# A planned order of 892 stages on one core: the old state added on VectorE, a square halved on GpSimd, and the last output row split

## The chip, the cores and the metric

The kernel runs on one core of one Trainium2 chip. The time is the device time of an execution in microseconds, and the figure that counts is the median of several executions. Five engines work beside each other and are bound to each other only by semaphores: PE (TensorE, matrix products), DVE (VectorE), ACT (ScalarE), POOL (GpSimd) and SP (SyncE, which here only issues transfers). Each runs its own instructions strictly in the order in which they were written.

## What is computed

Two layers follow each other. The first is a linear attention with a decaying state, for 4 batches, 8 heads, 768 time steps and a head size of 48. The second is a feed-forward layer from 384 to 1024 and back to 384, whose activation is h times softmax(h), followed by a layer norm.

```
state = 0
for t in range(S):
    cur = u * k[t] (outer) v[t]
    y[t] = r[t] @ (state + cur)
    state = w[t] * state + k[t] (outer) v[t]

h = y @ w_in                       # 3072 x 1024
solu = h * softmax(h)
ln = (solu - mean(solu)) / sqrt(var(solu) + 1e-6) * g_ln
out = ln @ w_out                   # 3072 x 384
```

## The kernel before, in words

The work is cut into 24 units: unit i is chunk c = i // 4 (128 time steps) of batch b = i % 4, with all 8 heads. A unit passes through about 35 small stages, and every stage is a Python function of a few instructions. What sets the order of everything is the string ORDER at the top of the file: 887 words, each a stage's short name, the unit's number and after a dot a choice. `Y13.i4`, for example, is the stage `attend` (Y) of unit 13, in form i, with PSUM bank 4; `kr2.d` is `transposed_copy` of unit 2 on DVE. The last lines of the kernel function walk through the words and call the stages. Each call goes through a small class (`InOrder`, its line 86 is what the profile gives for nearly every instruction), which ties each instruction to the one before it on the same engine, so that ORDER's order is the order on the engine; transfers issued by ACT and SP are kept in the words' order among each other too.

The stages that matter here, in the order in which one unit passes through them:

- LW, LK, LR, LV load w, k, r, v (192 KB each); the letter says whether SP (none), ACT (a) or POOL (g) issues the transfer.
- lw (ACT) takes the logarithm of w, cum (PE) sums it along time by two triangular products, ex (ACT) takes the exponential, kp (DVE) multiplies k and r with it. krk and krr (PE) transpose the results into PSUM, kr copies them to SBUF, on ACT or DVE. From unit 12 on, most units do this by a transposing transfer instead (kt, SP).
- p, q, dv (POOL) and dg (DVE) make the bonus term with u; vb casts v to bf16, on ACT or POOL.
- M (PE) makes the scores, m (mostly DVE) masks them into SBUF.
- Y (PE) makes y: old state times r, scores times v. In form i PE also adds the bonus term dv, by a product with the identity, and y is then copied by ACT; in form n it does not, and y is copied by DVE, which adds dv on the way.
- S (PE) adds the new part of the state in PSUM: a few tiny products for the decay, one product of the identity with the old state (384 columns, from chunk 1 on), and four products kp times v. et (ACT) takes the exponential of the decay, st (DVE) multiplies the sum with it and writes the new state in bf16, one of two buffers a batch.
- X (PE) transposes y and xT copies it to SBUF (ACT or DVE); some late units do this by a transposing transfer (xt, SP).
- H (PE) makes h, 24 products into two banks; e (ACT) is exp(h), he (DVE) is h times e, hq (ACT) is the square of he. In some late units ea (POOL) adds the two halves of e.
- Oa and Ob (PE) make the output for the first and the second four of the eight 128-row blocks of the hidden dimension: for each block one product of he with the weights (386 columns), one of e with a constant column (2 columns), and one of hq with a column of ones (1 column). In the units that have an ea, the e-products are only needed for every other block.
- qm (DVE), lv and rs (ACT) make the layer norm's factor, o (ACT or DVE) scales the row, out (SP) stores it. Units 17 to 20 use another form (ht), which does not matter here. Unit 23 makes its hidden part in two halves (HA to QB).

PSUM has eight banks, and the digit in a word says which one a stage takes; a stage that takes a bank waits until its last reader is done.

Of the kernel before, what the change touches and what calls it, by code (L numbers as in the profile page):

```python
# [21 lines left out]
LU0 LR3.g LW3.a LW1.a LW2.g lw3 LR0.a cum3.0 LG0 ih0 ex3 LW0 gs0.7 LK3 LR2.g hot1.2 LV0.g ik0 LK0 lw1 lw0 LV3.g
gc0 cum0.4 LK2.a us0.6 p0 lw2 LW5.g ex0 kp3 LR1 kp0 cum1.0 cum2.2 krk3.7 krr3 uc0 ex2 q0 ex1 kp2 LK1 LR6.g kp1
krk0.6 LW4 krr0 krk2.5 krr2 kr0.a lw4 LR4.g vb0.a kr2.d vb3.a p1 M0.3 p3 LO0 LW6 dg0 M2.5 kr3.a LK4 m0.d lw5
hot10.1 LV1 LR5 LK6.a dv0 LK5.g m2.d LV2.a LO1 M3.0 S0.7 q3 gw2.a gw3.a hot1.4 LI1 q1 lw6 krk1.6 cum4.2 et0 LV4
m3.d p2 st0 cum6.0 dg3 gw0.a cum5.4 ex4 S3.7 gw1.a p4 kp4 q2 dv3 krr1 ex6 dg1 LV5.g krk4.3 krr4 ex5 vb1.a Y0.i2
kp6 kr4.d y0.a LI2 et3 X0.2 krk6.3 st3 p6 kr1.a vb2.a LW8 xT0.a kp5 krr6 LI0.a dg2 M1.0 krk5.7 krr5 kr6.a m1.d
S1.2 dv1 M4.4 dv2 Y3.i3 S2.6 gw4.a LK7 gw7.a et2 kr5.d LW7.g et1 m4.d hot1.7 y3.a q4 gw6.a Y1.i3 M6.0 gw5.a st2
Y2.i5 y1.a y2.a vb5.a mn0.4 X2.7 wi0.a vb4.a st1 m6.d wi1.p LR7.g M5.2 X1.0 S5.1 xT2.a S4.6 et5 p5 lw7 LR8.g dg4
ce4.d LK8 LV7 et4 ce2.d wi2.a xT1.d st5 LW10.a st4 X3.5 m5.d LR10.a cum7.0 mc0 ex7 xT3.a ce1.d H0.6 dv4 H1.2 kp7  # L30
LK9.g H3.0 e0 lw8 e1 ce0.d LK10.a he0 he1 lw10 H2.6 ce7.d hq0.a ce3.p krk7.5 ce5.p e3 LV9 e2 LK11 hq1.a ce6.d
Oa0.3 q6 he3 vb7.a krr7 Ob0 LW9.g LV6.g Y4.i4 q5 LV8.g LR9.a he2 dg5 LW11 cum10.1 cum8.6 y4.a Oa1.0 qm0 ex10 lv0
rs0 kr7.d ex8 kp10 LW13.g Ob1 krk10.4 o0.a hq3.a p8 kp8 p7 dv5 Y5.n5 qm1 LR11.g y5.d lv1 M7.2 X4.6 LW15.a m7.d
q7 krr10 LW17 dg7 kr10.d xT4.a q8 dg6 rs1 lw11 p10 Oa3.5 o1.a cum11.6 dg8 hq2.a H4.2 LW12 LR12.a ex11 lw9 kp11
out0 S7.0 et7 Ob3 dv7 Y7.n1 vb6.a out1 cum9.6 LR17 LK15.g Oa2.4 qm3 st7 vb8.p e4 Ob2 he4 lv3 dv6 LK14.g krk8.0
S6.2 X5.3 LK12.a LV10 krr8 LV12.g ex9 lw13 y7.d rs3 o3.a hq4.a kp9 lw12 qm2 Y6.i5 lv2 xT5.d X7.7 krk11.6 LV11
vb9.p out3 kr8.d krr11 LR13.g LW14.a cum12.0 et6 xT7.a y6.a rs2 LR14.g st6 M8.2 krk9.5 krr9 kr11.d ex12 m8.a
H5.6 o2.d out2 q10 M11.3 LK13 lw17 kp12 dv8 LR15 S8.0 kr9.d LV15.g M9.1 e5 m11.d Oa4.5 LW18 Ob4 m9.a sel8 he5
LV14 et8 X6.6 vb11.a M10.3 st8 xT6.d p9 lw14 cum14.1 LK17.g hq5.a ex14 qm4 lv4 m10.d cum13.6 ex13 hot2.0 q9 rs4
kp14 kp13 dg9 Y8.i0 o4.a LW21.g dg10 sel9 Oa5.4 cum17.1 S9.3 LR16 lw15 p11 ex17 S11.5 cum15.6 Ob5 kp17 y8.a p12  # L40
et9 qm5 ex15 lv5 kp15 st9 dv9 Y9.n0 q11 q12 y9.d et11 rs5 H6.1 X8.6 o5.a p13 vb12.a p14 st11 dg11 kt12 e6 out4
dv11 LK21.g H7.3 X9.5 xT8.a he6 e7 LR19.g hq6.a vb10.a H8.6 lw18 krk14.0 LV16 dg12 krr14 dv10 kt15 xT9.d out5
he7 M12.1 Oa6.5 LV13.g Y11.n4 m12.d kr14.a e8 Ob6 M15.0 y11.d qm6 LR18 hq7.a lv6 he8 rs6 m15.d H9.3 dv12 o6.a
Y10.n2 y10.d e9 Oa7.7 he9 Ob7 LK19.g Y12.n0 S10.6 M14.2 LW16 X10.4 hq8.a LW22 y12.d qm7 xT10.d X12.5 Oa8.0 LV17
vb16.a out6 lw16 lv7 X11.1 LK16 hq9.a Ob8 xT12.a et10 p15 LR21 LK20.g LK18 cum16.4 m14.d q14 xT11.d cum18.2
vb14.a LR20.g dg14 rs7 st10 o7.a q15 qm8 S12.1 ex16 LW19.g LV18 LK22 H11.6 dg15 kp16 H12.4 vb15.p kt13 et12 ex18
lv8 vb13.p q13 e11 kp18 dv14 rs8 S15.2 o8.a S13.3 st12 e12 Oa9.0 dv15 he11 et15 lw21 LW20 Y15.n6 hq11.a et13
dg13 LV21 he12 Ob9 LV23.g LV19.g p18 st15 M13.4 LW23 y15.d qm9 dv13 kt16 cum21.1 hq12.a ex21 H10.6 lv9 p16 m13.d
st13 lw19 kp21 Y13.i4 Oa11.3 e10 rs9 o9.a out7 he10 q18 cum19.1 Ob11 dg18 qm11 lw20 Oa12.7 Ob12 ex19 LR22 q16
y13.a kp19 hq10.a M16.1 dg16 S14.5 lv11 Y14.n6 rs11 LV20.g X13.4 LV22.g out8 qm12 lv12 p17 m16.d xT13.d y14.d  # L50
o11.a lw22 S16.0 vb17.p et14 q17 dg17 rs12 st14 o12.a LR23 vb18.a cum20.1 p19 et16 ex20 ea10.p H13.3 q19 e13
xt15 dv17 lw23 kt17 dv16 H15.6 st16 kp20 he13 Oa10.5 xt14 M17.0 kt18 dg19 dv18 e15 cum22.2 Ob10 out9 ex22 vb22.p
Y16.i4 ea13.p he15 kp22 y16.a hq13.a p22 qm10 H14.6 vb20.p M18.3 m17.d p20 S18.2 q20 lv10 m18.d ea15.p e14 kt19
et18 rs10 Y17.n1 o10.a Oa13.0 y17.d kt20 p21 X16.4 Ob13 xT16.a st18 out11 q22 M19.3 xt17 he14 H16.1 hq15.a
Y18.n5 vb23.a e16 m19.d hq14.a Oa15.7 vb19.a dg20 kt21 y18.d qm13 out12 Ob15 ea14.p dv19 M20.4 q21 S17.3 lv13
he16 m20.d qm15 dv20 et17 hq16.a lv15 H17.1 rs13 out10 e17 M21.5 st17 xt18 rs15 ea16.p Oa14.4 m21.d Ob14 he17
o15.a o13.a cum23.5 qm14 LK23 Y20.n3 ex23 Y19.n7 lv14 y20.d y19.d H18.0 rs14 o14.a kp23 kt22 M22.3 e18 dg22
X20.2 vb21.p S19.7 m22.d xT20.a Oa16.6 Y21.n5 ht17 et19 p23 sv17 he18 xt19 hq17.a dv22 H20.2 e20 dg21 Ob16 st19
dv21 y21.d he20 hq18.a H19.0 qm16 e19 sv18 Y22.n4 Oa17.7 y22.d he19 kt23 Ob17 X22.5 sq17 M23.3 xT22.d qm17 m23.d
ht18 xt21 ht20 hq19.a lv16 Oa18.2 lv17 rs16 Ob18 ht19 q23 dg23 H21.0 o16.d sv19 Y23.n3 dv23 out15 hq20.a e21  # L60
y23.d H22.4 Oa20.6 out13 e22 Ob20 sq18 ea21.p Oa19.3 Ob19 he21 rs17 he22 hq21.a sq20 Oa21.1 o17.d sv20 out16
# [39 lines left out]
def kernel(  # L101
# [516 lines left out]
    def scaled_out(i, x):  # L618
        o_ps, rs, o = live[i]["o_ps"], rs_t[i % NWK], o_t[i % NWK]
        if x == "d":  # L620
            dve.tensor_scalar(out=o, in0=o_ps[:, :DM], scalar1=rs, scalar2=None, op0=MULT)
# [54 lines left out]
```

## Time and profile before

| what | value |
|---|---|
| median of 3 executions | 146.56 us (144.69, 146.56, 146.91) |
| the profiled execution, its own time | 145.05 us |
| its span from first to last instruction | 143.2 us |
| granted TensorE clock, mean | 0.995 |
| busy: PE / DVE / ACT / POOL | 127.6 / 124.0 / 122.2 / 117.2 us |
| bytes moved, mean rate | 31.67 MB, 221 GB/s |

The profile is of one execution. "Busy" is the time in which at least one record of an engine is open. Records of one engine overlap: the next instruction starts before the record of the one before it has ended, so the step from one start to the next is the better measure of what one more instruction costs. Matmuls are pipelined much more deeply than the rest, and there the difference is large. The view of stages gives, for each stretch of time, the busy time of each engine; the groups give mean durations; the timeline gives single instructions with the idle time before them and what ended it; the chain is followed back from the last instruction to what released each step.

### The profile page before, as it was taken

The numbers are of one execution on the slowest core, as the hardware profiler recorded it, in microseconds if no ns is written. First come the engines' busy times: TensorE is split into PE (matmuls) and PEld (weight loads), VectorE is DVE, ScalarE is ACT, GpSimd is POOL, SyncE is SP. The second block draws the span as 40 slices with busy tenths as digits, with TensorE's granted clock in tenths as the row PEclk, the third lists the DMA queues.
The fourth block names the chain that finished last, engine by engine and source line by source line (L and its number), as shares of the span: only waits on it lengthen the run. The fifth ranks groups of instructions, "written<-read, shape, count | busy, mean of one in ns | idle before, by whom it ended". The sixth has DMA issues, their size and how long they took to land.

```text
span 143.2 us, 4784 instructions
## 1 busy us (share of the span) xinstructions
PE 127.6 (89%) x1886; PEld 94.5 (66%) x1886; DVE 124.0 (87%) x206; ACT 122.2 (85%) x254; POOL 117.2 (82%) x150
## 2 busy tenths in 40 slices
PE   0597956988999999999999999996999999999980
PEld 0145445556967878678987797786778566687750
DVE  6048879979999999999999999999699999888480
ACT  3658799979999999999999989995787887887962
POOL 7999999999999999999999999999994753326000
PEclk9999999999999999999999999999999999999998
DMA  4999999999995999999998999996977863985325
GB/s 93 277 297 347 313 287 381 384 267 240 287 299 118 250 273 314 255 263 163 211 268 215 271 201 252 195 256 99 169 165 80 223 128 79 142 213 180 115 80 197
DMA packets 86488, 31.67 MB, mean 221 GB/s; under 512 B 80153, under 2 KB 84258, under 8 KB 86466
## 3 DMA queue, kind: packets, MB, share of 16 engines
q1 hardware_dynamic: 69330, 20.62, 66.6%
q0 software_dynamic: 2432, 7.47, 16.4%
q10 hardware_dynamic: 14704, 3.28, 10.5%
q8 instruction: 14, 0.23, 0.7%
q14 instruction: 8, 0.07, 0.1%
HBM read 22.03 MB, written 4.72 MB: 187 GB/s over the span
## 4 chain that ended last, share of the span: by engine, by line
PE 51%; POOL 21%; ACT 8%; issue 7%; DVE 5%; DMA 4%; ACTq 0%; POOLq 0%; DVEq 0%
PE ps L86 51%; DMA xT<-y 4%; POOL kr_in L86 4%; POOL p L86 4%; POOL q L86 3%; POOL dv L86 2%; POOL v_in L86 2%; ACT hq L86 2%; POOL w_in L86 2%; ACT e L86 2%; DVE he L86 1%; DVE o L86 1%; ACT o L86 1%; ACT ps L86 1%; DVE m L86 1%
## 5 line engine op out<-in xcount | busy, mean ns | idle before, releaser
L86 PE MATMUL ps<-w,he 128*128 128x386 bf16 (+1 forms) x192 | 42.5, 324 | 0.0
L86 PE MATMUL ps<-xT,win_sb 128*128 128x128 bf16 x480 | 29.6, 219 | 1.4 <-DMA xT<-y 1.2
L86 PEld LDWEIGHTS <-win_sb 128*128 128x128 bf16 x480 | 27.4, 98 | 3.0 <-DMA xT<-y 1.3
L86 POOL TENSOR_TENSOR dv<-vb,dg 128x384 bf16<-128x384 bf16 x24 | 19.8, 829 | 11.8 <-DVE dg L86 8.6
L86 DVE TENSOR_TENSOR kp<-ps,kr_in 128x768 bf16<-128x768 f32 x24 | 22.7, 953 | 6.9 <-DMA kr_in<-in_r_dram 3.8
L86 ACT ACTIVATE e<-ps 128x1024 bf16<-128x1024 f32 (+1 forms) x25 | 24.6, 987 | 4.8 <-PE ps L86 3.8
L86 DVE TENSOR_TENSOR m<-ps,keep 128x1024 bf16<-128x1024 f32 x22 | 26.7, 1218 | 0.9 <-PE ps L86 0.9
L86 DVE TENSOR_TENSOR he<-ps,e 128x1024 bf16<-128x1024 f32 (+1 forms) x21 | 24.5, 1170 | 3.0 <-ACT e L86 2.8
L86 PE MATMUL ps<-one_col,hq 128*128 128x1 bf16 x160 | 26.1, 163 | 0.0
L86 POOL TENSOR_TENSOR p<-kr_in 128x384 bf16<-128x384 f32 x24 | 23.9, 1005 | 0.1
L86 POOL TENSOR_TENSOR q<-p,u_bc 128x384 bf16<-128x384 bf16 x24 | 21.8, 916 | 0.3
L86 PEld LDWEIGHTS <-he 128*128 128x128 bf16 x192 | 18.3, 96 | 4.0
L86 ACT ACTIVATE hq<-he 128x1024 bf16<-128x1024 bf16 (+1 forms) x20 | 20.7, 1033 | 0.0
L86 ACT ACTIVATE ps<-ps 128x768 f32<-128x768 f32 x24 | 19.0, 800 | 1.5 <-PE ps L86 1.4
L86 PEld LDWEIGHTS <-hq 128*128 128x128 bf16 x160 | 14.1, 96 | 8.8
L86 PE MATMUL ps<-inv_col,e 128*128 128x2 bf16 x104 | 17.1, 164 | 0.0
L86 ACT ACTIVATE lw<-w_in 128x384 bf16<-128x384 f32 x24 | 12.3, 519 | 4.2 <-DMA w_in<-in_w_dram 4.2
L86 PEld LDWEIGHTS <-kp 128*128 128x128 bf16 x184 | 12.3, 101 | 4.2 <-DVE kp L86 1.9
L86 PEld LDWEIGHTS <-kr 64*128 64x128 bf16 (+1 forms) x272 | 10.2, 95 | 5.3 <-issue 2.1
L86 DVE TENSOR_REDUCE dg<-q 128x8 f32<-128x384 bf16 x24 | 12.9, 543 | 0.0
L86 DVE TENSOR_TENSOR st<-ps,et 128x384 bf16<-128x384 f32 x20 | 10.8, 551 | 1.4 <-ACT et L86 1.4
L86 POOL DMA_DIRECT2D v_in<-in_v_dram x12 | 10.9, 905 | 0.0
(97 smaller groups left out, 284.9 us busy)
## 6 DMA issues: line engine op xcount, KB each, us to landing
out_dram<-o SPq DMA_DIRECT2D x24, 192.0 KB, 2.7
w_in<-in_w_dram SPq DMA_DIRECT2D x12, 192.0 KB, 5.6
kr_in<-in_k_dram SPq DMA_DIRECT2D x12, 192.0 KB, 5.9
v_in<-in_v_dram POOLq DMA_DIRECT2D x12, 192.0 KB, 4.9
kr_in<-in_r_dram POOLq DMA_DIRECT2D x11, 192.0 KB, 4.5
v_in<-in_v_dram SPq DMA_DIRECT2D x11, 192.0 KB, 4.3
kr_in<-in_r_dram SPq DMA_DIRECT2D x9, 192.0 KB, 4.0
wout_f<-in_moe_w_out_dram SPq DMA_DIRECT2D x2, 768.0 KB, 7.1
```

What stands on the lines that cost most here:

```text
L86: made = make(*args, **kwargs)
```

## The change

ORDER is replaced by another one of 892 words. The same stages are called but for these:

- `S9.n3` and the like: in the units 9, 10, 13, 14, 18 and 19 the state's sum is made without the identity product of the old state. DVE adds the old state instead: it adds PSUM and the old state (bf16) into a new f32 buffer `sn` in SBUF, and then multiplies that buffer with the decay.
- `qa13.p` and the like: in the units 13, 14, 15, 16, 21 and 22 POOL adds the second half of hq to the first half (128x512), and Oa and Ob then need the one-column product for every other block only.
- `ea10.p` is gone: unit 10 makes all eight e-products again.
- `out23.h`: in the last unit ACT scales the left half of the row and DVE the right half, ACT and SP each store one half, and Ob23 runs all its he-products first, then those of e, then those of hq.
- Stages that change their engine: kr0, kr1, kr3, kr6 from ACT to DVE and kr2 from DVE to ACT; xT3, xT4, xT8 from ACT to DVE and xT1, xT11, xT13, xT22 from DVE to ACT; y6, y13 to DVE (form n), and y7, y14, y15, y17, y18 to ACT (form i, so with the identity product of dv); vb6, vb12, vb18, vb19 from ACT to POOL and vb17, vb21 from POOL to ACT; o2, o19, o20 from DVE to ACT and o18 from ACT to DVE.
- Many banks change, and nearly every compute stage stands at another place among its neighbours. In the word order the transfers of each issuing engine (SP 96, POOL 38, ACT 15) stand in the same order as before, apart from the split last store.

```diff
+    sn_t = ring("sn", 2, [C, H, D], F32)
...
-        s_ps = L["s_ps"] = bank([C, DM + H], F32, x, "s_ps")
+        s_ps = L["s_ps"] = bank([C, DM + H], F32, x[-1], "s_ps")
...
-        if c > 0:
+        L["apart"] = x[0] == "n"
+        if c > 0 and not L["apart"]:
             st = st_t[b][(c - 1) % 2]
             pe.matmul(s_ps[:, :DM], lhsT=ident, rhs=st.rearrange("p h e -> p (h e)"), start=False, stop=False,
                       skip_group_check=True)
...
-        dve.tensor_mul(out=st_t[b][c % 2], in0=live[i]["s_ps"][:, :DM].rearrange("p (h e) -> p h e", h=H), in1=et)
+        total = live[i]["s_ps"][:, :DM].rearrange("p (h e) -> p h e", h=H)
+        if live[i]["apart"]:
+            dve.tensor_add(out=sn_t[i % 2], in0=total, in1=st_t[b][(c - 1) % 2])
+            total = sn_t[i % 2]
+        dve.tensor_mul(out=st_t[b][c % 2], in0=total, in1=et)
...
+    def square_add(i, x):
+        hq = hq_t[i % NWK]
+        pool.tensor_add(out=hq[:, :KF // 2, :], in0=hq[:, :KF // 2, :], in1=hq[:, KF // 2:, :])
...
-            pe.matmul(o_ps[:, DM + 2:], lhsT=hq[:, f, :], rhs=one_col[:, :1], start=False, stop=(f == KF - 1),
-                      skip_group_check=True)
+            if i not in paired:
+                pe.matmul(o_ps[:, DM + 2:], lhsT=hq[:, f, :], rhs=one_col[:, :1], start=False, stop=(f == KF - 1),
+                          skip_group_check=True)
+            elif f % 2 == 0:
+                pe.matmul(o_ps[:, DM + 2:], lhsT=hq[:, f // 2, :], rhs=one_col[:, :1], start=False,
+                          stop=(f == KF - 2), skip_group_check=True)
...
+        if i == NU - 1 and split:
+            act.activation(out=o[:, :DM // 2], in_=o_ps[:, :DM // 2], func=COPY, scale=rs)
+            dve.tensor_scalar(out=o[:, DM // 2:], in0=o_ps[:, DM // 2:DM], scalar1=rs, scalar2=None, op0=MULT)
+            return
...
+        if x == "h":
+            act.dma_start(out=rows[:, :DM // 2], in_=o_t[i % NWK][:, :DM // 2])
+            sp.dma_start(out=rows[:, DM // 2:], in_=o_t[i % NWK][:, DM // 2:])
+            return
```

More of the change, by code (lines that the diff above doesn't have):

```diff
@@ L21 @@
 ORDER = """
[L22 to L61, printed above, removed]
@@ L62 @@
-hq22.a sq19 xt23 ea22.p out14 out17 qm18 qm20 qm19 lv18 HA23.5 rs18 o18.a EA23 DA23 lv19 HB23.7 rs19 out18 Ob21
-EB23 o19.d QA23.a qm21 DB23 lv20 QB23.d lv21 rs21 Oa22.4 Ob22 qm22 rs20 out19 Oa23.5 lv22 o21.d out21 rs22 o20.d
-Ob23 o22.a qm23 lv23 out22 rs23 out20 o23.a out23
+LU0 LW3.a LW1.a lw3 LR0.a LG0 LW0 lw0 LR3.g us0.0 LK3 gs0.5 cum3.2 gc0 uc0 LW2.g ih0 cum0.4 ex3 kp3 hot1.3 LR2.g
+LK0 LK2.a krk3.6 ex0 LV0.g ik0 lw2 cum2.2 kp0 LR1 LK1 ex2 LV3.g krk0.0 LW4 krr0 krr3 LO0 p0 LW6 kr3.d lw1 cum1.5
@@ new lines @@
+kp2 krk2.3 ex1 kr0.d LW5.g LK4 kp1 lw4 krr2 p2 LR6.g kr2.a vb0.a LV1 LR4.g M0.0 q0 hot1.4 M3.5 m0.d p3 krk1.4
+m3.d LR5 p1 lw5 LK5.g S0.0 q1 LK6.a krr1 LV2.a M2.6 dg0 gw3.a et0 q3 hot2.1 LO1 lw6 LI1 LV4 vb3.a kr1.d m2.d
+cum4.3 gw2.a cum5.6 ex4 cum6.1 q2 gw0.a LI2 dg3 LW8 dg2 kp4 hot10.5 ex6 dv0 st0 ex5 S3.0 kp6 et3 vb2.a dv3
+krk6.3 gw1.a LI0.a Y3.i1 p4 Y0.i5 LV5.g dg1 krr6 krk4.4 krr4 y3.a kp5 y0.a st3 kr6.d vb1.a gw4.a M1.1 q4 hot1.5
+dv2 dv1 Y2.i0 y2.a S2.7 LW7.g gw5.a m1.d M6.5 p6 wi1.p LR7.g p5 Y1.i0 m6.d gw6.a LR8.g S1.1 et2 LK7 dg4 LK8 LV7
@@ new lines @@
+kr4.d krk5.3 X2.2 st2 q6 krr5 gw7.a X3.5 y1.a vb4.a xT2.a LK9.g et1 kr5.d X1.4 xT1.a S4.0 M4.2 xT3.d X0.6 mn0.4
+st1 m4.d vb5.a wi0.a et4 M5.2 st4 ce2.d xT0.a lw7 wi2.a ce6.d LW10.a cum7.0 m5.d ce1.d LR10.a ce7.d dv4 mc0 S5.5
+lw8 ex7 H0.6 H1.2 kp7 e0 he0 ce4.d et5 H3.0 ce3.p e1 H2.6 LK10.a LV9 ce0.d krk7.4 st5 lw10 krr7 q5 he1 hq0.a
+LW9.g e3 e2 LV6.g ce5.p he3 Y4.i5 dg5 Oa0.3 hq1.a LK11 hq3.a he2 LV8.g LR9.a Ob0 qm0 cum10.1 ex10 Oa1.0 vb7.a
+cum8.6 LW13.g Ob1 p8 lv0 LW11 p7 y4.a rs0 o0.a kr7.d kp10 qm1 lv1 Oa3.5 ex8 q7 LW15.a LR11.g LW17 X4.4 M7.2 q8
@@ new lines @@
+LW12 Ob3 dg6 dg7 xT4.d vb9.p p10 vb6.p rs1 krk10.4 dv5 vb8.p lw11 kp8 krr10 LK15.g o1.a qm3 cum11.6 Y5.n1 hq2.a
+LR12.a ex11 lw9 LK14.g m7.d S7.0 lv3 lw17 dv7 H4.2 kr10.d lw12 y5.d kp11 et7 dg8 out0 st7 rs3 dv6 Oa2.4 e4 out1
+LV12.g cum9.6 LR17 LK12.a LV10 LR13.g he4 p11 krk8.1 LR14.g o3.a ex9 kp9 S6.0 krr8 et6 Ob2 LV11 Y7.i5 out3 q11
+krk9.2 lw13 lw15 kr8.d hq4.a X5.7 Y6.n3 LW14.a krk11.6 st6 LV15.g qm2 p9 dv8 krr11 y7.a lv2 rs2 o2.a cum12.0
+xT5.d y6.d out2 krr9 LK13 kr11.d ex12 X7.5 M8.3 kr9.d H5.6 kp12 m8.a LR15 LK17.g M11.3 xT7.a dg11 sel8 S8.0 M9.1
@@ new lines @@
+m11.d LW18 e5 Oa4.5 lw14 LW21.g he5 vb11.a et8 m9.a Ob4 X6.7 LV14 hq5.a st8 LR16 M10.3 xT6.d q9 dv11 m10.d
+cum14.1 cum13.6 q10 ex14 ex13 qm4 Y8.i0 kp14 kt12 Oa5.4 sel9 lv4 kp13 dg9 dg10 S9.n3 rs4 o4.a cum17.1 dv9 ex17
+S11.5 cum15.6 out4 kp17 y8.a Ob5 Y9.n0 LV16 ex15 qm5 vb10.a H6.1 lv5 et9 kp15 rs5 et11 p13 krk14.6 o5.a X8.7
+dv10 krr14 st9 p12 H7.3 e6 y9.d p14 kr14.a st11 X9.0 LK21.g LR19.g q12 xT8.d he6 H8.6 LV13.g e7 xT9.d hq6.a
+Y11.n2 M12.0 Oa6.5 he7 hq7.a e8 y11.d kt15 m12.d lw18 Ob6 dg12 out5 qm6 LR18 he8 vb12.p LW16 lv6 H9.2 rs6 LW22
@@ new lines @@
+vb14.a M15.0 Y10.n4 o6.a LV17 vb15.p m15.d S10.n7 out6 e9 Oa7.6 vb16.a he9 LK19.g Ob7 hq8.a Y12.n5 LK16 M14.1
+LR21 lw16 LK18 p15 LK20.g y10.d qm7 dv12 y12.d hq9.a lv7 rs7 LR20.g q15 LW19.g m14.d X10.4 Oa8.0 xT10.d et10
+dg15 vb13.p X11.5 Ob8 q13 LV18 st10 LK22 qm8 o7.a kt13 xT11.a lw21 X12.6 xT12.a cum16.4 p16 cum18.2 LW20 ex16
+lv8 dv15 LV23.g kp16 S12.1 LV19.g ex18 LV21 et12 H11.6 LW23 e11 kt16 out7 rs8 dg13 st12 H12.4 kp18 o8.a q14 e12
+q16 S13.n1 he11 cum21.2 Oa9.0 he12 Y15.i7 p18 hq11.a LR22 p19 out8 y15.a et13 st13 lw19 Ob9 qm9 M13.4 dv13 lv9
@@ new lines @@
+LV20.g H10.6 m13.d LR23 S15.1 ex21 xt15 e10 kt17 dg16 Oa11.5 vb17.a hq12.a Y13.n4 kp21 rs9 lw20 cum19.2 he10
+Ob11 y13.d ex19 qm11 Oa12.6 X13.4 o9.a Ob12 lv11 LV22.g p17 et15 dg14 xT13.a kp19 M16.2 st15 dv14 hq10.a q19
+rs11 S14.n7 cum20.0 o11.a Y14.i4 et14 y14.a qm12 vb20.p S16.5 dv16 lv12 et16 m16.d ex20 q18 H13.2 rs12 o12.a
+st14 dg19 Y16.i4 kp20 H15.6 e13 y16.a xt14 q17 lw22 st16 e15 kt18 p20 Oa10.5 dg17 he13 cum22.3 ex22 Ob10 hq13.a
+vb18.p M17.0 dg18 dv17 p21 he15 qm10 lv10 kp22 vb22.p dv18 out9 S18.n2 rs10 H14.6 ea13.p qa13.p et18 o10.a
@@ new lines @@
+hq15.a q21 M18.3 m17.d m18.d kt19 dg21 Y17.i5 kt20 X16.1 Oa13.0 y17.a xT16.a M19.4 st18 Ob13 out11 e14 H16.1
+lw23 Y18.i3 he14 xt17 e16 qm13 ea15.p m19.d qa15.p kt21 Oa15.7 vb19.p vb23.a he16 Ob15 dv19 ea14.p qm15 M20.5
+y18.a S17.4 lv13 m20.d hq14.a H17.1 et17 q20 M21.5 dg20 st17 Y19.n3 qa14.p hq16.a m21.d lv15 Oa14.4 rs13 e17
+out12 Ob14 dv20 rs15 out10 cum23.5 xt18 o13.a qa16.p he17 o15.a qm14 Y20.n7 p22 LK23 ea16.p ex23 kt22 p23 y19.d
+ht17 y20.d H18.0 lv14 e18 q22 vb21.a M22.2 kp23 X20.7 Oa16.6 rs14 xT20.a S19.n5 m22.d Ob16 sv18 dv21 H20.2 et19
@@ new lines @@
+he18 hq17.a q23 st19 dg22 xt19 dv22 kt23 e20 Y21.n7 o14.a y21.d dg23 qm16 H19.0 Y22.n5 ht18 Oa17.7 e19 he20
+y22.d Ob17 M23.4 xt21 ht20 X22.3 lv16 Oa18.2 he19 ht19 rs16 dv23 sq17 H21.0 m23.d hq20.a hq19.a xT22.a Y23.n4
+o16.d Ob18 H22.5 e21 sv17 hq18.a y23.d Oa20.4 Ob20 qm17 sq18 he21 qm18 e22 Oa19.3 ea21.p lv17 he22 sv19 lv18
+hq21.a rs17 out15 Ob19 sq20 out13 hq22.a o17.d out16 rs18 xt23 ea22.p sv20 sq19 HB23.1 HA23.6 qm20 qa21.p lv20
+out14 Oa21.0 qm19 EA23 qa22.p lv19 o18.d Ob21 DA23 rs20 rs19 o19.a out17 EB23 qm21 lv21 DB23 rs21 QA23.a Oa22.5
@@ L65 @@
+out18 Ob22 qm22 lv22 rs22 o21.d QB23.d o20.a o22.a Oa23.1 out19 out21 Ob23 qm23 out22 lv23 rs23 o23.d out20
+out23.h
 """
@@ L540, in hidden_square @@
             dve.scalar_tensor_tensor(out=hq, in0=he, scalar=EPS * EPS, in1=he, op0=MULT, op1=MULT)
+    paired = {int(word[2:].split(".")[0]) for word in ORDER.split() if word.startswith("qa")}
+    def square_add(i, x):
+        hq = hq_t[i % NWK]
+        pool.tensor_add(out=hq[:, :KF // 2, :], in0=hq[:, :KF // 2, :], in1=hq[:, KF // 2:, :])
     def hidden_half(part):
@@ L568 @@
     first_half, second_half = hidden_half(0), hidden_half(1)
+    split = "out23.h" in ORDER.split()
     def output(i, part):
@@ L572, in output @@
         e, he, hq, o_ps = e_t[i % NWK], he_t[i % NWK], hq_t[i % NWK], L["o_ps"]
+        if i == NU - 1 and part and split:
+            for f in range(KF // 2, KF):
+                pe.matmul(o_ps[:, :DM + 2], lhsT=he[:, f, :], rhs=w2[:, f, :], start=False, stop=False,
+                          skip_group_check=True)
+            for f in range(KF // 2, KF):
+                pe.matmul(o_ps[:, DM:DM + 2], lhsT=e[:, f, :], rhs=inv_col, start=False, stop=False,
+                          skip_group_check=True)
+            for f in range(KF // 2, KF):
+                pe.matmul(o_ps[:, DM + 2:], lhsT=hq[:, f, :], rhs=one_col[:, :1], start=False, stop=(f == KF - 1),
+                          skip_group_check=True)
+            return
         for f in range(part * KF // 2, (part + 1) * KF // 2):
@@ L584, in output @@
                           skip_group_check=True)
-            pe.matmul(o_ps[:, DM + 2:], lhsT=hq[:, f, :], rhs=one_col[:, :1], start=False, stop=(f == KF - 1),
-                      skip_group_check=True)
+            if i not in paired:
+                pe.matmul(o_ps[:, DM + 2:], lhsT=hq[:, f, :], rhs=one_col[:, :1], start=False, stop=(f == KF - 1),
+                          skip_group_check=True)
+            elif f % 2 == 0:
+                pe.matmul(o_ps[:, DM + 2:], lhsT=hq[:, f // 2, :], rhs=one_col[:, :1], start=False,
+                          stop=(f == KF - 2), skip_group_check=True)
     def output_a(i, x):
@@ L626, in store @@
         c, b = units[i]
-        queue[x].dma_start(out=out[b * S + c * C:b * S + (c + 1) * C, :], in_=o_t[i % NWK])
+        rows = out[b * S + c * C:b * S + (c + 1) * C, :]
+        if x == "h":
+            act.dma_start(out=rows[:, :DM // 2], in_=o_t[i % NWK][:, :DM // 2])
+            sp.dma_start(out=rows[:, DM // 2:], in_=o_t[i % NWK][:, DM // 2:])
+            return
+        queue[x].dma_start(out=rows, in_=o_t[i % NWK])
     stages = dict(
@@ L635 @@
         Y=attend, y=y_copy, S=state, et=state_decay, st=state_update, X=x_transposed, xT=x_copy,
-        H=hidden, e=hidden_exp, he=hidden_mul, ea=hidden_add, hq=hidden_square, Oa=output_a, Ob=output_b,
+        H=hidden, e=hidden_exp, he=hidden_mul, ea=hidden_add, qa=square_add, hq=hidden_square, Oa=output_a, Ob=output_b,
         sq=sums, qm=variance, lv=scale, rs=root, o=scaled_out, out=store,
```

## The prediction, made before the changed kernel ran

> **What bounds the kernel now.** I read the page's totals first, then the stages, then the chain, then single instructions.
>
> ```profile
> PE 127.6 (89%) x1886; PEld 94.5 (66%) x1886; DVE 124.0 (87%) x206; ACT 122.2 (85%) x254; POOL 117.2 (82%) x150
> ```
>
> Four engines lie within ten microseconds of each other, so the total names no bound. The stages do; columns are PE, PEld, DVE, ACT and POOL busy.
>
> ```profile
> 10.00:47.00 37.00, 31.85 (x460) 23.28 (x458) 34.54 (x48) 34.33 (x66) 36.52 (x42) 1.00 1.08 293
> 47.00:99.00 52.00, 50.82 (x864) 41.07 (x863) 50.87 (x81) 50.03 (x102) 51.50 (x61) 1.00 1.10 235
> 99.00:130.00 31.00, 31.00 (x455) 22.30 (x453) 28.41 (x41) 24.24 (x53) 18.64 (x23) 1.00 0.77 153
> 130.00:143.20 13.20, 8.97 (x106) 6.19 (x103) 6.91 (x15) 8.77 (x26) 1.82 (x2) 0.95 0.37 129
> ```
>
> From 10 to 99 us DVE is idle for 2.46 + 1.13 = 3.6 us, POOL for 0.48 + 0.50 = 1.0 us: both are full, and PE waits for them in small pieces. From 99 to 130 us PE has no idle time at all while POOL rests for 12.4 us. After 130 us comes a tail. So work put on DVE before 99 us is dear, on POOL after 99 us free, and what PE is spared counts in full only after 99 us. The chain shows where the two regimes meet:
>
> ```profile
> 92.53 6.12 DMA xT<-y
> 98.65 0.05 issue
> 98.70 31.40 PE ps L86 x456
> ...
> 139.81 0.58 ACT o L86
> ```
>
> A transposing transfer of y (unit 15) lands at 98.65 us, PE goes on and does not stop for 31.4 us; ACT's last o ends at 140.4 us, and 2.8 us later the span is over.
>
> **PE: what a product really costs.** Timeline of PE, columns start and length:
>
> ```profile
> 84.44 0.32 PE L86 MATMUL ps<-st,ident 128*128 128x384 bf16 x1
> 84.60 0.33 PE L86 MATMUL ps<-vb,kp 128*128 128x96 bf16 x4
> ...
> 85.39 0.17 PE L86 MATMUL ps<-inv_col,e 128*128 128x2 bf16 x1
> 85.42 0.16 PE L86 MATMUL ps<-one_col,hq 128*128 128x1 bf16 x1
> 85.44 0.32 PE L86 MATMUL ps<-w,he 128*128 128x386 bf16 x1
> ```
>
> ```profile
> L86 PE MATMUL ps<-one_col,hq 128*128 128x1 bf16 x160 | 26.1, 163 | 0.0
> L86 PE MATMUL ps<-st,ident 128*128 128x384 bf16 x16 | 5.2, 323 | 0.0
> L86 PE MATMUL ps<-dv,ident 128*128 128x384 bf16 x9 | 3.0, 329 | 0.2 <-ACT y L86 0.2
> ```
>
> The group says 163 ns for a one-column product, but the next product starts 0.02 to 0.03 us later (85.42 to 85.44): records overlap, and dropping one saves about 0.025 us. The identity product of the old state steps by 0.16 us (84.44 to 84.60), half of its 323 ns. Hence on PE:
> - six units halve the hq-products: 6 x 4 x 0.025 = -0.6 us, all after 99 us.
> - six state sums lose the identity product: 6 x 0.16 = -0.96 us, of which units 18 and 19 (-0.32) lie after 99 us.
> - five Y go to form i (7, 14, 15, 17, 18), two to form n (6, 13): +3 x 0.16 = +0.5 us, of which 17 and 18 (+0.32) after 99 us.
> - the e-products of unit 10 come back: +4 x 0.025 = +0.1 us.
>
> Sum -1.0 us on PE, and -0.6 us where PE is the bound. By the records' lengths it would be 24 x 0.163 + 6 x 0.32 - 3 x 0.33 - 4 x 0.16 = 4.2 us, which I take for an illusion.
>
> **DVE: what is added.**
>
> ```profile
> L86 DVE TENSOR_TENSOR st<-ps,et 128x384 bf16<-128x384 f32 x20 | 10.8, 551 | 1.4 <-ACT et L86 1.4
> L86 DVE TENSOR_TENSOR y<-ps,dv 128x384 bf16<-128x384 f32 x15 | 8.2, 551 | 1.1 <-POOL dv L86 1.1
> L86 DVE TENSOR_SCALAR o<-ps,rs 128x384 f32<-128x384 f32 x6 | 3.6, 608 | 0.0
> ```
>
> ```profile
> 13.18 0.68 DVE L86 COPY kr<-ps 128x1024 bf16<-128x1024 bf16 x1
> 13.77 0.54 DVE L86 TENSOR_REDUCE dg<-q 128x8 f32<-128x384 bf16 x1
> ...
> 16.95 1.23 DVE L86 TENSOR_TENSOR m<-ps,keep 128x1024 bf16<-128x1024 f32 x1 [0.37 <-PE ps L86]
> ...
> 32.17 1.04 DVE L86 TENSOR_TENSOR st<-ps,et 128x384 bf16<-128x384 f32 x2 [0.78 <-ACT et L86]
> ...
> 89.41 0.55 DVE L86 TENSOR_TENSOR st<-ps,et 128x384 bf16<-128x384 f32 x1
> 89.87 0.95 DVE L86 TENSOR_TENSOR kp<-ps,kr_in 128x768 bf16<-128x768 f32 x1
> ...
> 101.31 1.22 DVE L86 TENSOR_TENSOR he<-ps,e 128x1024 bf16<-128x1024 f32 x1 [1.00 <-ACT e L86]
> ```
>
> Steps again, not lengths: st steps by 0.46 us (89.41 to 89.87), a copy of kr by 0.59 us (13.18 to 13.77). The new add of the old state has the shape of y's add. But the multiplication behind it needs its result, so the pair can't overlap as neighbours do: the add costs between 0.46 (the step) and about 0.65 (its 0.55 whole and 0.1 for the hand-over, my estimate from the difference of length and step); I take 0.58. The multiplication now reads SBUF instead of PSUM; I leave it at 0.46. Up to about 101 us:
> - adds of units 9, 10, 13, 14: 4 x 0.58 = +2.3 us
> - copies of kr, three more: 3 x 0.59 = +1.8 us
> - y: two come, three go (7, 14, 15): -0.46 us
> - o2 goes: about 0.52 (0.608 less the same overlap of 0.09): -0.5 us
> - xT: three come, three go: 0
>
> Sum +3.1 us, against 3.6 us of idle time before 99 us and the 1.00 us at 101.3. After that DVE gains as much as it loses (two adds come; y17, y18, xT22 and one o net go), and it has 2.6 us of room to 130 us. What can pay for the 3.1 us: the waits on PE and ACT in the first 47 us (0.37 and 0.78 above) follow from ACT, which makes kr in 1.01 us and is relieved of three; I count 1.5 us of the 2.46 as recovered. The 1.00 us wait at 101.3 (for unit 15's e, behind the transfer that lands at 98.65) is worth 1.0: DVE may come that much later without anybody noticing, as the transfers keep their order. That leaves +0.6 us, between -0.5 (nearly all idle time used) and +2.1 (only the last 1.0 recovered).
>
> **POOL, ACT and the queues.**
>
> ```profile
> L86 POOL TENSOR_TENSOR ea<-e 128x512 bf16<-128x512 bf16 x7 | 8.0, 1148 | 1.4 <-ACT e L86 0.9 <-ACT sq L86 0.6
> L86 POOL TENSOR_TENSOR q<-p,u_bc 128x384 bf16<-128x384 bf16 x24 | 21.8, 916 | 0.3
> L86 ACT COPY kr<-ps 128x1024 bf16<-128x1024 bf16 x5 | 5.1, 1012 | 0.2 <-PE ps L86 0.2
> ```
>
> The new adds on POOL have ea's shape: 6 x 1.15 = 6.9 us, all after 99 us and covered by its 12.4 us of rest there and the 11.4 us behind. They add a wait: the first hq-product of Oa waits for POOL, and behind it on PE waits everything else. If POOL is late there, each unit can cost PE up to 1.15 us; the order puts four or more PE stages between (for unit 21 the two halves HB23 and HA23), so I take 0. Casts of vb (two more) and ea10 (gone) cancel before 99 us. SP, ACT and POOL issue the same transfers in the same order, so no queue is passed: 0.
>
> **The tail.**
>
> ```profile
> L86 DVE TENSOR_TENSOR he<-ps,e 128x1024 bf16<-128x1024 f32 x19 | 23.1, 1221 | 1.7 <-ACT e L86 1.5
> L86 DVE TENSOR_TENSOR he<-ps,e 128x512 bf16<-128x512 f32 x2 | 1.4, 687 | 1.4 <-ACT e L86 1.4
> out_dram<-o SPq DMA_DIRECT2D x24, 192.0 KB, 2.7
> ```
>
> 512 columns less save 0.53 us, so 192 less save 0.2 us of the last o. The last store of 192 KB takes 2.7 us; at the 129 GB/s of the last stage its half would land 0.8 us sooner, and nothing if it is all latency: I take 0.3. Together -0.5 us.
>
> **The sum** against the profiled execution (145.05 us; span 143.2 and 1.85 around it): -0.6 (PE) + 0.6 (DVE) - 0.5 (tail) = -0.5 us, 144.5 us. That execution is the second fastest of the four times known; the three runs have a median of 146.56 and the four a mean of 145.8. I put the forecast between the two bases: 145.3 us, no change.
>
> **Rivals.**
> 1. *The two operands in SBUF (slower).* No DVE instruction of before reads two large SBUF operands while POOL works; the new multiplications of `sn` by the decay do. If such an instruction must wait for the POOL instruction in hand, it loses between 0 and 0.92 us (q's row), 0.46 in the middle, and POOL as much. Units 9, 10, 13 and 14 lie where POOL is busy 51.5 of 52 us: 4 x 0.46 = +1.8 us, at the most +3.7: 147.1 to 149.0 us. From 0.3 us each on it eats the 1.26 us between the forecast and the median of before. For it: both engines are full there. Against it: nothing in the trace. The Trainium skill, page "SBUF — State Buffer", section "Who interferes with whom", says that a VectorE instruction with two SBUF inputs contends with a GpSimd instruction that reads SBUF, and that the later one fully blocks; by it this rival would hold and the time be the 147.1 us above; no row of before can show it.
> 2. *DVE stays full (slower).* None of the 3.1 us is recovered but the 1.0 at 101.3: 145.3 + 1.5 = 146.8, and 147.8 if that too is lost. For it: a DVE that is idle 1.13 of 52 us. Against it: ACT is relieved early.
> 3. *The order packs better (faster).* DVE's idle time falls by all of the 3.1 us, so the 99 us point comes 1 us earlier, PE's 1.2 us of idle in the stage before go too: 145.3 - 1.0 - 1.2 = 143.1 us. For it: 2.5 us of idle on DVE in the first 47 us. Against it: transfers keep their times, and the one landing at 98.65 holds unit 15 where it is.
> 4. *Records' lengths count on PE:* 145.3 - 3.6 = 141.7 us. The steps above speak against it.
>
> **Chances.** Forecast 0.42 (144.0 to 146.6), rival 1 0.22, rival 2 0.14, rival 3 0.19, rival 4 0.03. The range that leaves out about two in ten reaches from rival 3 to the upper part of rival 1: 142.8 to 148.6 us. A change of 2% is about what this kernel's measurement can tell from none, 143.6 and 149.5 us. Below the first lie most of rival 3 and rival 4: 0.20. Above the second lies the end of rivals 1 and 2: 0.14. The rest is 0.66.
>
> **What would show it.** Steps: products of hq that step by 0.025 us and are 136 instead of 160; DVE busier than 98% from 47 to 99 us; the pair add and multiplication stepping by 1.04 us in units 9 to 14 (over 1.3 us, with POOL's instruction ending just before the multiplication starts, means rival 1); H of unit 15 released by the transfer or by nothing, at 98 to 99.5 us; PE without idle time from there; the last store's halves landing sooner than 2.7 us. I am wrong if PE idles after 99 us for POOL's halved squares, or if the first 47 us move by more than 1.5 us either way.

## The result, and the profile after

The changed kernel takes 152.05 us (median of 5, 151.09 to 153.09) against 145.93 us of the kernel before (5 runs): 1.045 times as long, 95% interval 1.035 to 1.055. The forecast was 145.3 us in a range of 142.8 to 148.6. The profiled execution of the changed kernel took 152.05 us with a span of 150.3 us, so 7.1 us more span than before. Ratios and their intervals are taken from undisturbed executions alone, the medians from all.

The view of stages of the changed kernel, with the same columns and edges as before (busy time of PE, PEld, DVE, ACT, POOL):

```profile
10.00:47.00 37.00, 30.00 (x421) 21.86 (x421) 32.57 (x47) 29.97 (x57) 34.90 (x40) 1.00 1.05 284
47.00:99.00 52.00, 48.63 (x815) 38.88 (x814) 51.24 (x77) 45.87 (x92) 48.00 (x57) 1.00 1.03 232
99.00:130.00 31.00, 29.86 (x439) 21.38 (x437) 30.74 (x44) 25.21 (x58) 28.26 (x32) 1.00 0.74 130
```

Up to 47 us every engine is less busy than before (DVE 32.57 us against 34.54, ACT 29.97 against 34.33): there the engines wait more. From 47 us on, DVE is busy 98.5% and 99% of the time, and in the first of these stages with fewer instructions than before (77 after 81): its instructions have become longer. The stage after 99 us, which was PE's, is now DVE's.

Matching DVE's instructions of the two traces one by one (the order of the words names each) shows where the time is lost:

| instruction of DVE | start before | start after | later by |
|---|---|---|---|
| kp of unit 7 | 34.78 | 37.60 | 2.8 |
| kp of unit 17 | 64.70 | 67.07 | 2.4 |
| y of unit 9 | 67.25 | 72.27 | 5.0 |
| m of unit 13 | 88.28 | 94.22 | 5.9 |
| he of unit 15 | 101.31 | 107.13 | 5.8 |
| he of unit 20 | 122.77 | 129.52 | 6.8 |
| last instruction of the kernel (span) | 143.2 | 150.3 | 7.1 |

Two jumps make up most of it: one before 35 us, and one between 67 and 72 us, followed by smaller ones. The second stands just at the first new multiplication. The groups of DVE in the changed kernel, with the mean in ns behind the comma:

```profile
L87 DVE TENSOR_TENSOR st<-sn,et 128x384 bf16<-128x384 f32 x6 | 8.7, 1453 | 0.2
L87 DVE TENSOR_TENSOR st<-ps,et 128x384 bf16<-128x384 f32 x14 | 7.6, 545 | 0.0
L87 DVE TENSOR_TENSOR sn<-ps,st 128x384 f32<-128x384 f32 x6 | 3.3, 546 | 0.4 <-ACT et L87 0.4
```

The multiplication that reads both operands from SBUF takes 1453 ns, the same one out of PSUM 545 ns: 6 x 0.91 = 5.4 us, on top of six adds. What it waited for is seen when the timelines of DVE and of POOL are laid side by side. DVE, units 9, 10 and 19:

```profile
69.57 2.77 DVE L87 TENSOR_TENSOR st<-sn,et 128x384 bf16<-128x384 f32 x1
72.27 0.54 DVE L87 TENSOR_TENSOR y<-ps,dv 128x384 bf16<-128x384 f32 x1
...
85.33 1.13 DVE L87 TENSOR_TENSOR st<-sn,et 128x384 bf16<-128x384 f32 x1
...
127.37 0.56 DVE L87 TENSOR_TENSOR st<-sn,et 128x384 bf16<-128x384 f32 x1
```

POOL in the same stretches:

```profile
69.20 0.82 POOL L87 TENSOR_TENSOR dv<-vb,dg 128x384 bf16<-128x384 bf16 x1
69.98 1.94 POOL L87 TENSOR_TENSOR p<-kr_in 128x384 bf16<-128x384 f32 x2
...
85.04 1.00 POOL L87 TENSOR_TENSOR p<-kr_in 128x384 bf16<-128x384 f32 x1 [0.66 <-DMA kr_in<-in_k_dram]
86.00 1.15 POOL L87 TENSOR_TENSOR dv<-vb,dg 128x384 bf16<-128x384 bf16 x1
...
126.56 0.91 POOL L87 TENSOR_TENSOR q<-p,u_bc 128x384 bf16<-128x384 bf16 x1
128.47 0.83 POOL L87 TENSOR_TENSOR dv<-vb,dg 128x384 bf16<-128x384 bf16 x1 [1.00 <-DVE dg L87]
```

In unit 9 POOL's three instructions end at 71.92 us and DVE's record ends 0.42 us later, at 72.34: about the time the multiplication itself needs. In unit 10 POOL's p ends at 86.04 and DVE's record at 86.46, again 0.42 us later; the dv behind it takes 1.15 instead of 0.83 us, so POOL then waits for DVE. In unit 19 POOL's q ends 0.1 us after the start and nothing of POOL follows for a microsecond: 0.56 us. No wait stands in the profile's brackets for any of it, only the record is longer: here two engines are bound to each other by something other than a semaphore. The trace also shows that `sn` in SBUF is not slow by itself, since unit 19 reads it too and takes 0.56 us.

The first jump is found on ACT, followed by the DVE instruction that needs its result:

```profile
33.12 1.03 ACT L87 CAST win_sb<-win_f 128x1024 bf16<-128x1024 f32 x1
...
35.97 0.48 ACT L87 CAST mean_sb<-ps 128x384 bf16<-128x384 f32 x1 [1.82 <-DVE w L87]
36.34 0.53 ACT L87 ACTIVATE lw<-w_in 128x384 bf16<-128x384 f32 x1
36.77 0.80 ACT L87 ACTIVATE ps<-ps 128x768 f32<-128x768 f32 x1
```

```profile
34.81 1.13 DVE L87 SCALAR_TENSOR_TENSOR w<-wout_f,gr,ps 128x384 bf16<-128x384 f32 x2
37.60 0.96 DVE L87 TENSOR_TENSOR kp<-ps,kr_in 128x768 bf16<-128x768 f32 x1 [1.67 <-ACT ps L87]
```

ACT's copy of the column mean (`mc0`) reads a PSUM bank that DVE's corrections `ce` read too. Neither needs the other's result, but the program makes the later one in the words wait for the earlier. In the old words `mc0` stood behind ce4 and ce2, which DVE ran at 30.0 us, and it started without a wait (DVE's row, then ACT's, of the kernel before):

```profile
30.00 1.13 DVE L86 SCALAR_TENSOR_TENSOR w<-wout_f,gr,ps 128x384 bf16<-128x384 f32 x2
```

```profile
33.44 0.50 ACT L86 CAST mean_sb<-ps 128x384 bf16<-128x384 f32 x1
```

In the new words it stands behind ce2, ce6, ce1 and ce7, the last of which ends at 35.9 us. ACT stands idle for 1.82 us, and behind the copy wait ex7, kp7 and with them the next PE work.

### The profile page after: what moved, and what is told of

Its sections match the earlier page's. It is cut to its first block, busy times and chain, and to the rows that moved or that the text cites. A ratio compares the mean times of both kernels' runs of the same rounds, so it can differ in the third digit from the quotient of the medians.

```text
span 150.3 us, 4744 instructions
## 1 busy us (share of the span) xinstructions
PE 128.8 (86%) x1863; PEld 95.0 (63%) x1863; DVE 132.3 (88%) x210; ACT 120.8 (80%) x255; POOL 124.8 (83%) x157
## 4 chain that ended last, share of the span: by engine, by line
PE 40%; DVE 27%; POOL 14%; issue 8%; ACT 6%; DMA 3%; DVEq 0%; POOLq 0%; ACTq 0%
PE ps L87 40%; DVE kp L87 5%; DVE m L87 4%; DVE he L87 4%; DVE st L87 3%; POOL kr_in L87 3%; DMA xT<-y 3%; POOL q L87 3%; DVE dg L87 3%; POOL p L87 2%; ACT ps L87 1%; DVE w L87 1%; DVE sn L87 1%; DVE y L87 1%; ACT e L87 1%
## 5 line engine op out<-in xcount | busy, mean ns | idle before, releaser
L87 PE MATMUL ps<-one_col,hq 128*128 128x1 bf16 x136 | 21.8, 163 | 0.0
L87 PEld LDWEIGHTS <-he 128*128 128x128 bf16 x192 | 16.9, 96 | 2.6
L87 PEld LDWEIGHTS <-hq 128*128 128x128 bf16 x136 | 12.8, 96 | 8.8
L87 PE MATMUL ps<-inv_col,e 128*128 128x2 bf16 x112 | 18.0, 164 | 0.0
L87 PEld LDWEIGHTS <-kp 128*128 128x128 bf16 x184 | 11.7, 101 | 5.8 <-DVE kp L87 2.8
L87 PEld LDWEIGHTS <-kr 64*128 64x128 bf16 (+1 forms) x272 | 10.8, 95 | 6.0 <-issue 2.9
L87 PEld LDWEIGHTS <-e 128*128 128x128 bf16 x112 | 10.6, 96 | 2.2 <-issue 1.3
L87 POOL TENSOR_TENSOR ea<-e 128x512 bf16<-128x512 bf16 x6 | 6.9, 1151 | 5.9 <-ACT e L87 5.9
```

The lines of the kernel that those rows point to most:

```text
L87: made = make(*args, **kwargs)
```

## The experiments

Each kernel is compared with the kernel before on the same chip; that one's median lay between 145.02 and 146.16 us from chip to chip, so the ratios count. The changed kernel's own comparison was against 145.93 us.

**The sum kept in PSUM.** Edit of the changed kernel:

```diff
-            dve.tensor_add(out=sn_t[i % 2], in0=total, in1=st_t[b][(c - 1) % 2])
-            total = sn_t[i % 2]
+            dve.tensor_add(out=total, in0=total, in1=st_t[b][(c - 1) % 2])
```

> The changed kernel, but the add of the old state writes its sum back into PSUM, so that the multiplication with the decay reads PSUM and one SBUF operand instead of two SBUF operands; DVE runs the same instructions in the same order. Theory A (the multiplication with two SBUF operands waits for GpSimd's instruction in hand): the six multiplications fall from 1.45 us on average to about 0.55, DVE is relieved of 5.4 us, and the time falls by 3.5 to 5 us, to 147 to 148.5 us. Theory B (DVE is simply too full, each added instruction lengthens the time): nothing changes, 152 us. Theory C (the first 47 us are what counts): nothing changes, 152 us.

Measured: 147.85 us, 1.018 of the kernel before (1.012 to 1.024). DVE's timeline in the same place:

```profile
69.04 0.56 DVE L87 TENSOR_TENSOR ps<-ps,st 128x384 f32<-128x384 f32 x1
69.63 0.56 DVE L87 TENSOR_TENSOR st<-ps,et 128x384 bf16<-128x384 f32 x1
70.11 0.55 DVE L87 TENSOR_TENSOR y<-ps,dv 128x384 bf16<-128x384 f32 x1
```

The same instructions in the same order, one operand from PSUM instead of SBUF: the pair steps by 1.07 us. Of the 4.5 per cent that the change cost, 2.7 are gone (3.9 us; 4.2 by the bare medians). Theory A as forecast; B and C alone are out.

**The copy of the mean ahead.** Edit of the words of the changed kernel; each engine's own order stays as it was:

```diff
-ce6.d LW10.a cum7.0 m5.d ce1.d LR10.a ce7.d dv4 mc0 S5.5
+ce6.d LW10.a cum7.0 LR10.a mc0 m5.d ce1.d ce7.d dv4 S5.5
```

> The changed kernel, but the words are interleaved so that ACT's copy of the column mean comes before two of DVE's four corrections that read the same PSUM bank; every engine's own order stays the same, only which of the two waits for the other is turned around. In the changed kernel ACT sat idle for 1.82 us before that copy. Theory C (the lag of 2.4 us at the end of the first 40 us comes from this wait): the copy starts at 34.1 instead of 36.0 us, everything behind it comes about 1.8 us sooner, 150.2 us. Theory A alone or theory B alone (a DVE or GpSimd that is full afterwards swallows it): 151.5 to 152 us.

Measured: 150.26 us, 1.036 (1.029 to 1.043). The copy now follows ACT's instruction before it at once:

```profile
33.16 1.03 ACT L87 CAST win_sb<-win_f 128x1024 bf16<-128x1024 f32 x1
...
34.10 0.47 ACT L87 CAST mean_sb<-ps 128x384 bf16<-128x384 f32 x1
```

That is 1.8 us less by the bare medians, which is the length of the wait, and 1.3 us by the ratios, whose intervals overlap. The trace is clearer: `kp` of unit 17 starts 0.6 us later than in the kernel before instead of 2.4, and the span is 2.0 us shorter than the changed kernel's, although DVE is full afterwards. The delay ahead of the full engine was not made up in the changed kernel.

**Both.**

> Both edits together: the sum in PSUM and the copy of the column mean ahead. If A and C both hold and are independent, 145.3 to 146.7 us (3.5 to 5 us and 1.8 us less than 152.05). If B holds, still above 150 us.

Measured: 145.77 us, 1.0036 (1.0004 to 1.0067). These three kernels ran on one chip, so their medians can be compared: with the sum in PSUM the copy ahead is worth 2.1 us (147.85 to 145.77), with the copy ahead the sum in PSUM is worth 4.5 us (150.26 to 145.77). Together the two causes explain all but about half a microsecond of the loss. The stage from 47 to 99 us of this kernel:

```profile
47.00:99.00 52.00, 51.44 (x877) 41.78 (x875) 51.21 (x81) 49.18 (x101) 50.97 (x62) 1.00 1.11 233
```

DVE is as busy as in the changed kernel (51.21 and 51.24 us), but carries 81 instructions instead of 77 and feeds PE for 51.44 instead of 48.63 us. The busy time alone couldn't tell work from waiting.

**No add at all.** The words S9.n3, S10.n7, S13.n1, S14.n7, S18.n2, S19.n5 of the changed kernel without their n.

> The changed kernel with the identity product of the old state back on TensorE in all six units and no add on DVE; everything else as changed. Theory A: as the sum in PSUM (147 to 148.5 us) or up to 2 us less, since six adds of 0.47 us go as well and 1 us of products comes back: 146 to 148 us. Theory B (only the added work counts, not the wait): 152.05 less 2.8 us, 149 to 150 us.

Measured: 147.55 us, 1.016 (1.009 to 1.022), the same as with the sum in PSUM within the intervals. So the six adds themselves hardly cost anything here; the wait did.

**The add alone, in the old order.** The words of the kernel before, with n in those six S.

> The kernel before, its order untouched, with one part of the change alone: in the six units 9, 10, 13, 14, 18 and 19 the old state is added by DVE into the SBUF buffer and multiplied from there. Theory A (the multiplication with two SBUF operands waits for GpSimd): the six multiplications take 1 to 1.5 us instead of 0.55 wherever GpSimd is working, and the time grows by 3 to 5 us, to 148 to 150 us. If the wait needs the changed order (GpSimd's instructions standing just there), at most 1 us more: 146 us.

Measured: 149.83 us, 1.027 (1.022 to 1.032). DVE in unit 9, and POOL beside it:

```profile
67.38 2.49 DVE L86 TENSOR_TENSOR st<-sn,et 128x384 bf16<-128x384 f32 x1
69.80 0.55 DVE L86 TENSOR_TENSOR y<-ps,dv 128x384 bf16<-128x384 f32 x1
```

```profile
65.78 1.77 POOL L86 TENSOR_TENSOR q<-p,u_bc 128x384 bf16<-128x384 bf16 x2
67.52 1.94 POOL L86 TENSOR_TENSOR p<-kr_in 128x384 bf16<-128x384 f32 x2
```

The effect needs nothing of the new order. Here too the multiplication gets through only behind two further instructions of POOL that began after it. In unit 13 of this run it took 1.26 us although POOL did nothing there but issue two transfers (DVE's row, then POOL's):

```profile
94.25 1.26 DVE L86 TENSOR_TENSOR st<-sn,et 128x384 bf16<-128x384 f32 x1
```

```profile
93.91 1.80 POOL L86 DMA_DIRECT2D v_in<-in_v_dram  x2
```

So POOL's elementwise instructions are not all that such a multiplication can lose time beside. This is a single case, and its cause was not tested.

**The same with the sum in PSUM.**

> As the kernel before with the six adds, but the sum is written back into PSUM, so that no DVE instruction reads two SBUF operands: the price of the added DVE work by itself. Theory A: six adds of about 0.5 us on DVE against 1 us of products saved on PE: 145 to 146.5 us. Theory B (DVE full, all of it shows): 145.0 plus 2.8, 147.8 us.

Measured: 146.03 us, 1.002 (0.999 to 1.006). Six adds on DVE against six products spared on PE are no difference that can be measured. Theory B is out: a DVE that is 98% busy took them in.

**The halved squares alone, in the old order.** The words of the kernel before, with qa behind hq in the units 13, 14, 15, 16, 21 and 22.

> The kernel before, its order untouched, with GpSimd's halving of the squares alone, in the units 13, 14, 15, 16, 21 and 22, each add placed right behind the square in the words. By the step between products (0.025 us for each of 24) 0.6 us less: 144.4 us. If PE comes to wait for GpSimd's add instead: 145 to 147 us. By the length of the records (0.163 us each) it would be 141 us.

Measured: 152.54 us, 1.045 (1.038 to 1.051); all three expectations missed. Two rows of PE's waits, and the stage after 99 us of this kernel:

```profile
PE ps L86 <- POOL hq L86: 3.4, 2, 2.7
...
PE ps L86 <- POOL ea L86: 0.5, 1, 0.5
```

```profile
99.00:130.00 31.00, 26.12 (x352) 17.92 (x353) 23.61 (x33) 21.07 (x44) 22.35 (x25) 0.94 0.62 116
```

PE stands idle for 4.9 of 31 us in a stage in which it had no idle time before. One add of POOL's accounts for 2.7 us of it; 0.5 us went to an `ea` and 1.4 us to a transposing transfer. That one wait, for unit 15's add, ends at 116.14 us, and from 117 to 120 us the granted clock was 0.50, the 6 in the page's row of forty slices:

```profile
PEclk9999999999999999999999999999999699999999
```

Matched with the kernel before, DVE's `he` of unit 16 is 3.1 us late and that of unit 17 is 7.9 us late. So 4.8 of the 8.3 us by which this span is longer arise in one place, more than the wait itself; that the low clock makes up the rest is likely but not shown. POOL had fallen behind by then: it stood idle before the first add, which is placed right behind a square that ACT had not yet made, and worked without a break from there on:

```profile
107.53 1.15 POOL L86 TENSOR_TENSOR hq<-hq 128x512 bf16<-128x512 bf16 x1 [3.28 <-ACT hq L86]
```

In the changed order this wait doesn't occur: no row there has PE waiting for POOL's hq. The new order hides the piece; whether another place for the adds in the old order would do so too was not tried. (One execution's profile; it also started 1.3 us late behind a load.)

**The last row in one piece,** on the kernel with both repairs.

> The kernel with the sum in PSUM and the copy of the column mean ahead (145.77 us), and the last row scaled and stored in one piece by DVE and SP again, with the old order of products in the last unit. In the changed kernel the two halves of the scaling ran one after the other (0.42 us each, DVE's starting when ACT's had ended) instead of 0.58 us. If the split gains what I forecast (0.5 us), this takes 146.3 us; if the loss of 0.3 us and the shorter store cancel, 145.8; if only the loss counts, 145.4.

Measured: 146.65 us on a chip on which the kernel before took 146.16: 1.003 (0.999 to 1.007), against 1.0036 with the split. No gain of the split is to be seen, though two intervals of about half a per cent each way could hide the 0.5 us forecast. In the changed kernel its halves ran one after the other:

```profile
146.91 0.42 ACT L87 ACTIVATE o<-ps,rs 128x192 f32<-128x192 f32 x1
...
147.37 0.42 DVE L87 TENSOR_SCALAR o<-ps,rs 128x192 f32<-128x192 f32 x1 [0.96 <-ACT o L87]
```

Again two readers of one PSUM bank, put in a row by the program (they also write two halves of one tile, and which of the two is the reason was not tested). The scaling takes 0.88 us instead of 0.58, and from the last scaling to the end of the span it is 2.5 us instead of 2.8: the one takes back what the other gives.

**Taking pieces out of the repaired kernel.** Without the halved squares:

> The kernel with the sum in PSUM and the copy of the column mean ahead (1.0036 of the kernel before), without GpSimd's halving of the squares: 24 one-column products come back to PE, 6.9 us of GpSimd's work go. By the step between products: 0.6 us more, 1.008 of the kernel before. If GpSimd's adds cost PE waits even in this order: 1.000 or less.

Measured: 1.0054 (1.0018 to 1.0091), 146.70 us.

Without the add on DVE:

> The changed kernel with the identity product of the old state back on PE in all six units, no add on DVE, and the copy of the column mean ahead. Against the kernel with the sum in PSUM and the mean ahead (1.0036): DVE is spared six adds of about 0.5 us, PE gets 1 us of products. If DVE is the tighter engine in that stretch: 1 us less, 0.997. If PE is: 0.5 us more, 1.007.

Measured: 1.0015 (0.998 to 1.005), 146.01 us, between the two expectations.

Without all three pieces:

> What is left of the change when all three new pieces are taken out (no add on DVE, no halving of squares, the last row in one piece) and the copy of the column mean stands ahead: the new order and the stages that change their engine. If the order is as good as the old one and the pieces bring little: 0.995 to 1.005 of the kernel before. If the new pieces carry the order (it was made for them): over 1.01.

Measured: 1.012 (1.008 to 1.016), 147.09 us. The intervals of the first two overlap, and both ratios lie within the interval of the repaired kernel. Leaving the halving out costs 0.3 us by the ratios, with 0.6 forecast, and that is not to be told from nothing. The bare order is worse than the old one by a per cent, as expected if the new pieces carry the order; where it loses the time was not looked for. None of these versions is faster than the kernel before.

## Why the prediction was wrong, step by step

- **"The multiplication now reads SBUF instead of PSUM; I leave it at 0.46"** is the step that failed. Its step was 0.48 us in unit 19 only and 1.05 to 2.70 in the others. The mechanism stood there as rival 1, with a chance of 0.22, and was mis-sized: half of one POOL instruction (0.46 us) for four units, 1.8 us in all. The runs show 0.9 us on average for six, 5.4 us on DVE and 3.9 to 4.5 us of time, which is more than the 3.7 us put down as the most, since the multiplication waits for the rest of one to three POOL instructions, and since POOL's later stage is not empty enough either (units 14 and 18 lost 0.66 and 1.0 us after 99 us). The rule of the Trainium skill that was cited beside it ("SBUF — State Buffer", section "Who interferes with whom") names the contention, and there the trace agrees: 0.56 us with POOL done 0.1 us after the start, 1.13 to 2.77 beside a busy one, and POOL's next instruction 0.32 us longer in unit 10. Its rule that the later instruction is the one that is blocked did not hold in unit 9, where two of POOL's instructions began after DVE's and still went first.
- **"I count 1.5 us of the 2.46 as recovered" before 47 us** failed in sign: the order lost 1.8 us there, by the wait of `mc0` for ce7. I had added up each engine's work and not read which words stand between two readers of one bank. The diff shows it: the old words have mc0 ahead of ce1, the new ones behind ce7. The prediction's own sign of being wrong, a move of more than 1.5 us in the first 47, came true. With the copy ahead `kp` of unit 17 is 0.6 us late, so once that wait was gone most of the 1.8 us of added copies of kr was indeed recovered; what failed was to leave the wait out.
- **DVE's added work, +3.1 us, largely hidden**: right. The six adds cost nothing that can be measured (1.002 alone in the old order), and the remainder after both repairs is 0.4%.
- **PE's products by steps of 0.025 and 0.16 us, -1.0 us in all and -0.6 where it counts**: the counts came out (136 products of hq), and the gain is too small to be told from nothing in these runs. The reading by the records' lengths (4.2 us) is out: no version gained anything like it.
- **POOL's adds at 0 in the new order**: right for PE, which never waits for them; two small DVE instructions in the tail grew by 1.3 us together beside them (last section), which the time without the adds doesn't show. The price without cover was put at up to 1.15 us a unit; alone in the old order they cost about 6.4 us in all, most of it at one unit.
- **The tail, -0.5 us**: by the trace it is 0, since the halves don't run beside each other; the times are too coarse to tell.
- **The 1.00 us wait at 101.3 us as a cushion**: DVE has no wait there any more, but what the cushion was worth can't be read off, since by then everything was 6 us late.

The range missed because it was drawn around one mechanism at a time; rival 1 at its upper end and a late ramp together are 145.3 + 3.7 + 1.8 = 150.8 us, which still falls short of the 152.05. Still open is what decides whether DVE gets through behind one POOL instruction or only behind three. A lead stands in the three traces with `sn` in SBUF: all six POOL instructions that began after DVE's and went first were p's, which read f32, while the dv and q that were next in line, in bf16, gave way and became longer (1.15 and 1.23 us in the changed kernel). Whether the type is the reason was not tested. Also open is where the last 0.4% of the repaired kernel lies.

## What to carry to other kernels

Moving an operand from PSUM to SBUF can cost more than the instruction: before an elementwise operation of VectorE gets a second SBUF operand, look at what GpSimd does at that place, and keep one operand in PSUM if GpSimd is busy there. When an order is rewritten, list for each PSUM bank the readers on different engines and which one stands first, because a wait between two readers needs no data to exist. And a new piece that is free in an order made for it may cost six microseconds in another, most of them in a single place, so price it together with the words around it.

## What the runs showed of the hardware that was not expected

- A VectorE multiplication of 128x384 with both operands in SBUF took 0.56 us where GpSimd was done 0.1 us after its start, and up to 2.77 us beside three back-to-back instructions of it (0.82, 0.99 and 0.99 us), two of which began after it.
- No semaphore row of the profile shows such a wait. It stands there as busy time of the waiting engine, so DVE read 51.24 us busy of 52 with 77 instructions done instead of 81.
- The small differences of one column (qm of the units 17 to 20, also with two SBUF operands), not touched by the change, grew with it: their mean was 153 ns before and 468 ns after, since POOL's halved squares of the last units now run beside two of them:

```profile
139.46 1.69 DVE L87 TENSOR_TENSOR qm<-s,sq 128x1 f32<-128x1 f32 x2
```

```profile
138.88 2.26 POOL L87 TENSOR_TENSOR hq<-hq 128x512 bf16<-128x512 bf16 x2 [0.25 <-ACT hq L87]
```

Two of them took 1.69 us together and DVE's next work came when POOL's second instruction was over, at 141.1 us.
